# Bucketed attention into a capacity-routed mixture of experts: X's transposes in the maxima's tiles, sums of v in four column positions, and another order of the first expert's loads and subtractions

## The chip, the cores and the metric

One core of a Trainium2 chip runs the whole program. The metric is device time of one execution in microseconds, the median of several runs. TensorE (PE, with PEld for its weight loads), VectorE (DVE), ScalarE (ACT) and GpSimd (POOL) each work through their own queue in order; SyncE (SP) and GpSimd issue the DMAs.

## The reference

```python
def _attn_ref(q, k, v, proj):            # q, k, v: 4 x 8 x 768 x 64, proj: 64 x 6
    q_bits = (q @ proj > 0); k_bits = (k @ proj > 0)
    mask = q_bucket[..., :, None] == k_bucket[..., None, :]     # buckets: six bits each
    scores = np.where(mask, scale * q @ k.T, -1e9)
    attn = np.exp(scores - scores.max(-1, keepdims=True))
    return attn / (attn.sum(-1, keepdims=True) + 1e-9) @ v

def _moe_ref(x, w_gate, w1, w2):         # x: 3072 x 512, 8 experts, 512 -> 1024 -> 512
    # all (token, expert) logits are taken from the largest down; a token goes to the first
    # expert that still has room (384 each)
    out[mask] = np.maximum(x[mask] @ w1[e], 0) @ w2[e]
```

## The kernel before

**Attention.** The 32 heads (4 batches of 8) are taken in order, six key blocks of 128 each: 192 steps, numbered t. A step issues, in an order written out by hand, the transposed scores of one key block in two halves (`ST`, into a ring of three PSUM tiles `psT`, with the exponential on ScalarE), the row maxima of a later head (`S_pass`, into a ring of two tiles `psS` of two banks each, reduced on VectorE), the low halves of the probabilities (`lo`, mostly on GpSimd) and, four steps later, the product with v (`AV`). Everything in 32 bits is split into a high and a low half of 16. Other work is put into the steps by half-step numbers n = 2t: the lists `P1` to `P4` give the numbers at which the q, k and v of the next group of four heads are cast (`cast`, `cv`), subtracted (`sub`, `sv`), projected onto the hash bits (`bits`), moved by DMA to the layout that the scores use (`moves`) and summed over keys (`sumv`). For the second group (G=1) `moves` comes in three parts at half-steps 23, 24 and 28. The loads of a group's q and k go into tiles with one buffer, on SyncE's queue, which also issues the moves.

`sumv` multiplies a 128x128 matrix `on`, zero but for ones in two columns, with the 64 columns of v of four heads at once (256 columns, six blocks, high and low), so that rows 97 and 98 of one PSUM tile hold the sums; one copy on ScalarE and one operation on VectorE take rows 96 to 127 out.

After every second head `xtr` transposes its 128 columns of the attention's output X, three row blocks a call and two calls two half-steps apart, in tiles of `psT`; ScalarE copies the high half, VectorE subtracts the low one. `logits` multiplies them with the gate.

**Experts.** Each expert takes 68 pieces of matmuls: 32 of the first layer, 36 of the second (three blocks c of 128 members, twelve pieces each). Beside the pieces of one expert runs the routing of the next (`phase`), a chain of some ten to fourteen steps through VectorE and TensorE, put at piece numbers `E1`, `E2` and `EV`. The weights are gathered by GpSimd's indirect DMAs (`wload`), cast by ScalarE to their high half (`wsplit`), and the low half is subtracted in halves of a quarter, 128x512 each. These subtractions wait in a list `pend`: `hand` takes the next few of it at a routing step, behind a one-element copy (`tick`) that keeps GpSimd from running ahead of the step; the lists `hs` say how many at each step, and what has not been handed out by a piece number `by` is issued there. For the first expert the first half of w1 is loaded before the routing ends, the second half and w2 (two halves) behind a tick on the gathered and split X.

Of the kernel before, what the change touches and what calls it, by code (L numbers as in the profile page):

```python
# [27 lines left out]
 P1=[13, 14, 15, 16, 17, 18, 20, 21, 16, 24, 21, 26, 23, 24, 33, 32, 3, 2, 46, -1, -1, 13],  # L28
 P2=[41, 44, 48, 49, 51, 51, 57, 55, 45, 49, 55, 57, 52, 60, 59, 51, 1, 4, 63, 32, 36, 47],
 P3=[69, 73, 82, 80, 84, 86, 89, 86, 75, 83, 87, 90, 94, 96, 97, 99, 2, 3, 115, 58, 62, 87],  # L30
# [12 lines left out]
def attention(tc, nc, ctx, qT, kT, vv, proj, wg, x_dram, L, jp, identf, B, late=None, after=None):  # L43
# [64 lines left out]
    wc=row(97,768.0,"wc"); ml=row(98,-1.0,"ml")  # L108
    on=cp.tile([128,128],F16,name="on"); G_.memset(on,0.0); G_.memset(on[:,97:99],1.0)
    ident=cp.tile([128,128],F16,name="ident"); V.tensor_scalar(ident,jp,0.0,None,op0=ALU.is_equal)  # L110
# [51 lines left out]
    def moves(G,part=0):  # L162
# [4 lines left out]
        def go(dst,src,r0=0):  # L167
            for r,js in hs: SY.dma_start(dst[u][r0:r0+64,js,0:S],src[r])
# [7 lines left out]
        if part==1: todo=(go,QA,h[0]),(go,KA,h[1]),(signs_,)  # L176
        elif part==2: todo=(go,QB,h[0]),(nxt,0),(go,KB,h[1],64),(nxt,1)
        elif part==3: todo=()
        else: todo=(go,QA,h[0]),(go,QB,h[0]),(nxt,0),(go,KA,h[1]),(go,KB,h[1],64),(signs_,),(nxt,1)
        for f,*x in todo: f(*x)  # L180
        if part in (0,3): go(KB,l[1]); go(QB,l[0],64)
    def clear(G):
# [4 lines left out]
    def sumv(G):  # L187
        u=G%2
        if G<2:
            V.tensor_copy(WF[u][96:128,:,64],wc[96:128,:].to_broadcast([32,4]))  # L190
        ps=psT.tile([128,512],F32,name="pst")
        pv=ps[96:128,0:256].rearrange("p (j d) -> p j d",j=4)
        n=0
        for c in range(6):
            for src in (VH[u],VL[u]):
                T.matmul(ps[:,0:256].rearrange("p (j d) -> p j d",j=4),on,src[:,:,c,0:64],start=n==0,stop=n==11,skip_group_check=True); n+=1
        hi=dp.tile([128,4,64],F16,name="shi",bufs=1)
        A.copy(hi[96:128],pv)
        V.scalar_tensor_tensor(WF[u][96:128,:,0:64],hi[96:128],ml[96:128],pv,op0=ALU.mult,op1=ALU.add)

# [89 lines left out]
    def wsplit():  # L290
        A.copy(wgs[:,:,0],wgr); G_.tensor_tensor(wgs[:,:,1],wgr,wgs[:,:,0],op=ALU.subtract)
    def xtr(b,d,hf):
        ps=psT.tile([128,512],F32,name="pst"); p=ps[:,0:384].rearrange("p (c q) -> p c q",c=3); r=slice(3*hf,3*hf+3)
        for c in range(3):
            T.transpose(p[:,c],X[b][:,3*hf+c,d*128:d*128+128],identf)
        A.copy(XH[:,d,r],p)
        V.tensor_tensor(XL[:,d,r],p,XH[:,d,r],op=ALU.subtract)  # L297
# [49 lines left out]
    for h in range(1,NH,2):  # L347
        b,d=h//8,h%8//2; n=2*(6*h+5+LAG)+AP['X'][0]
        if h==NH-1: n=2*(6*h+5+LAG)
        for hf in range(2): add(n+AP['X'][1]*hf,xtr,b,d,hf)  # L350
        if b==B-1: add(n+4,logits,b,[d])
# [43 lines left out]
W2=[2,4,7,11]  # L395
W10=[(2,4),(3,6)]
W20=[9,12,15,18]
XS=[57,57,60,63]
# [3 lines left out]
class Moe:  # L402
# [399 lines left out]
    def start(s):  # L802
# [3 lines left out]
        next(s.ph0)  # L806
        s.gather(0)
        s.wsplit(0,0,0,V)
        next(s.ph0)
# [4 lines left out]
        s.gate=s.W[0,'x'][0][0:1,0,256:257].bitcast(F32); s.tick()  # L814
        s.wload(0,0,4,(2,3))
        s.wload(0,1,2)

    def run(s):
# [7 lines left out]
        for p in range(1,8):  # L826
# [3 lines left out]
            hs=[0]*(len(ev)-10)+HS  # L830
            if p==1: hs=[0,0,0,0,0,2,2,2,2,2,0,1,1,0]
            if p==2: hs=[0,2,3,2,3,2,0,0,4,0]
            if p==7: ev=ev[-2:]; hs=[0,0]
# [6 lines left out]
        for k in range(8):  # L840
            for q in range(4): add(NS*k+(W2 if k else W20)[q],s.wsplit,k,1,q,None,NS*k+(BY[2] if k else 42) if k<6 else 0)
            for n in SC: add(NS*k+n,s.scatter)
        for q,n in W10: add(n,s.wsplit,0,0,q,None,8*q-2)
        for n in range(-NS,NS*8):
# [59 lines left out]
```

## Time and profile before

| | |
|---|---|
| median of 3 runs | 765.25 us (764.78 to 770.71) |
| profiled execution | 768.65 us, of which the span of instructions is 766.8 |
| mean granted TensorE clock | 0.966 of full |
| TensorE busy | 698.3 us (91%) |
| VectorE busy | 562.9 us (73%) |
| GpSimd busy | 547.7 us (71%) |
| ScalarE busy | 403.2 us (53%) |

The profile is of one execution; its times run from the span's first instruction. A matmul's length includes its way through the array, so two matmuls in a row overlap: starts tell more than lengths. Attention ends at about 412 us, the first expert's matmuls begin at about 442 and the second's at about 490.

### The profile page before, as it was taken

Reading aid. Unit: us, or ns where it says so; the run is one execution under the profiler, and the core shown is the slowest. Engines: PE = TensorE matmul, PEld = TensorE weight load, DVE = VectorE, ACT = ScalarE, POOL = GpSimd, SP = SyncE. Lnnn points to the kernel's source line nnn. Section 1 sums busy time; section 2 is a strip of 40 time slices with the busy share of each in tenths; the row PEclk is TensorE's granted clock in tenths of the full one; section 3 lists DMA queues with packets and bytes.
Section 4 is the critical chain, followed back from the end, with each engine's and each line's share of the span. In section 5 each row is a group of like instructions: output and inputs, shape, how many; then the busy total and the mean of one; then the engine's idle time right before and its main releaser. Section 6 shows DMA issues by size and latency. Waiting matters only on the chain. (4 is left out here: it accounts for less than half of the span.)

```text
span 766.8 us, 19086 instructions
## 1 busy us (share of the span) xinstructions
PE 698.3 (91%) x7748; PEld 544.0 (71%) x7748; DVE 562.9 (73%) x1318; ACT 403.2 (53%) x788; POOL 547.7 (71%) x467
## 2 busy tenths in 40 slices
PE   7898898999999999998887687989999999999995
PEld 2566675767767676675665576877988888988894
DVE  6788978889888898987765687778888888843120
ACT  5776676777776777655562141614343434333430
POOL 7694969696886968765662375768787887887761
PEclk7899999999999999999997599999999999999998
DMA  8539655426454273420000343434262626262511
GB/s 206 147 96 220 149 157 123 121 74 166 129 122 123 80 190 98 105 58 23 22 22 23 97 166 111 165 138 151 86 217 77 227 67 237 59 244 97 207 39 42
DMA packets 40000, 93.57 MB, mean 122 GB/s; under 512 B 4597, under 2 KB 30569, under 8 KB 37865
## 3 DMA queue, kind: packets, MB, share of 16 engines
q1 hardware_dynamic: 33048, 46.21, 23.2%
q0 software_dynamic: 6784, 46.14, 17.2%
q8 instruction: 61, 1.00, 0.6%
q14 instruction: 27, 0.21, 0.1%
q10 hardware_dynamic: 80, 0.00, 0.0%
HBM read 59.53 MB, written 12.58 MB: 94 GB/s over the span
## 5 line engine op out<-in xcount | busy, mean ns | idle before, releaser
L258 POOL TENSOR_TENSOR lo<-pt 128x768 f16<-128x768 f32 x143 | 233.5, 1646 | 78.0 <-ACT pt L255 68.6
L255 ACT ACTIVATE pt<-pst 128x384 f32<-128x384 f32 x384 | 182.9, 491 | 98.6 <-PE pst L254 87.7
L231 DVE TENSOR_REDUCE m<-pss 128x1 f16<-128x770 f32 x192 | 182.6, 956 | 42.3 <-PE pss L229 41.3
L253 PE MATMUL pst<-qa,ka 128*128 128x384 f16 x384 | 125.6, 327 | 6.8 <-DVE XT L297 4.0
L254 PE MATMUL pst<-qb,kb 128*128 128x384 f16 x384 | 125.5, 327 | 1.1 <-DMA qb<-ql 1.1
L270 PE MATMUL psv<-vh,lo 128*128 128x65 f16 x1152 | 121.1, 194 | 1.8 <-POOL lo L258 1.8
L269 PE MATMUL psv<-vl,pt 128*128 128x64 f16 x1152 | 121.3, 193 | 0.0
L268 PE MATMUL psv<-vh,pt 128*128 128x65 f16 x1152 | 121.2, 194 | 0.0
L743 POOL TENSOR_TENSOR wl<-wf,wh 128x512 fp32r<-128x512 f32 x92 | 115.8, 1278 | 0.0
L268 PEld LDWEIGHTS <-pt 128*128 128x128 bf16 x1152 | 106.7, 98 | 12.7 <-issue 3.1
L269 PEld LDWEIGHTS <-pt 128*128 128x128 bf16 x1152 | 105.8, 99 | 9.5
L229 PE MATMUL pss<-ka,qa 128*128 128x385 f16 x384 | 95.4, 331 | 17.2 <-DVE m L231 14.6
L270 PEld LDWEIGHTS <-lo 128*128 128x128 f16 x1152 | 105.8, 97 | 2.0 <-POOL lo L258 1.9
L731 ACT CAST wh<-wf 128x1024 fp32r<-128x1024 f32 x64 | 65.1, 1048 | 38.3 <-DMA wf<-in_w_dram,zwidx 37.8
L779 ACT ACTIVATE hh<-ph 128x384 fp32r<-128x384 f32 x64 | 31.4, 491 | 83.3 <-PE ph L777 83.3
L229 PEld LDWEIGHTS <-qa 128*128 128x128 f16 x384 | 37.6, 98 | 50.4 <-issue 26.5
L780 DVE SCALAR_TENSOR_TENSOR hl<-ph,hh 128x384 fp32r<-128x384 f32 x64 | 35.3, 556 | 41.5 <-ACT hh L779 41.0
L777 PE MATMUL ph<-xh,wh 128*128 128x384 f32 x256 | 60.1, 349 | 3.3 <-DVE hl L780 3.0
L258 DVE TENSOR_TENSOR lo<-pt 128x768 f16<-128x768 f32 x49 | 61.6, 1258 | 1.5 <-ACT pt L255 1.0
L792 ACT COPY o<-po 128x512 f32<-128x512 f32 x24 | 14.1, 587 | 82.4 <-PE po L789 80.9
L777 PE MATMUL ph<-xl,wh 128*128 128x384 f32 x256 | 56.8, 340 | 0.0
L777 PE MATMUL ph<-xh,wl 128*128 128x384 f32 x256 | 56.1, 339 | 0.0
(263 smaller groups left out, 1418.1 us busy)
## 6 DMA issues: line engine op xcount, KB each, us to landing
vp<-in_vv_dram SPq DMA_DIRECT2D x8, 768.0 KB
x_dram<-X SPq DMA_DIRECT2D x16, 384.0 KB
qp<-in_qT_dram SPq DMA_DIRECT2D x7, 768.0 KB
kp<-in_kT_dram SPq DMA_DIRECT2D x7, 768.0 KB
qa<-qh SPq DMA_DIRECT2D x14, 192.0 KB
ka<-kh SPq DMA_DIRECT2D x14, 192.0 KB
qb<-qh SPq DMA_DIRECT2D x14, 192.0 KB
kb<-kh SPq DMA_DIRECT2D x14, 192.0 KB
```

Source lines behind the costliest of these rows:

```text
L229: T.matmul(ps[:,hf,0:HK],QA[u][:,j,qc*128:qc*128+128],KA[u][:,j,hf*HK:hf*HK+HK],start=True,stop=True)
L231: V.tensor_reduce(M6[h][:,qc:qc+1],ps[:,:,0:HK],axis=AX.XY,op=ALU.max,negate=True)
L253: T.matmul(ps[:,0:384],KA[u][:,j,kr],QA[u][:,j,r],start=True,stop=False)
L254: T.matmul(ps[:,0:384],KB[u][:,j,kr],QB[u][:,j,r],start=False,stop=True)
L255: A.activation(PT[h,kc][0][:,r],ps[:,0:384],AF.Exp,scale=0.125)
L258: eng.tensor_tensor(l,p,p.bitcast(BF)[:,1::2],op=ALU.subtract)
L268: T.matmul(av[:,c,:],ph[:,r],VH[u][:,j,kc,:],start=(kc==0 and c==0),stop=False,skip_group_check=True)
L269: T.matmul(av[:,c,0:64],ph[:,r],VL[u][:,j,kc,:],start=False,stop=False,skip_group_check=True)
L270: T.matmul(av[:,c,:],l[:,r],VH[u][:,j,kc,:],start=False,stop=False,skip_group_check=True)
L731: s.nc.scalar.copy(h[:,r],f[:,r])
L743: for _ in range(n): s.nc.gpsimd.tensor_tensor(*s.pend.pop(0)[1],op=ALU.subtract)
L777: T.matmul(p[:,0:384],a[:,o:o+128],b[:,d],start=n==0,stop=n==11)
```

## The change

In attention: `xtr2` takes all six row blocks of a pair of heads in one tile of `psS`, for the first three batches (twelve calls); the last batch keeps `xtr`. `sumv` uses a 128x32 matrix with ones in columns 1 and 2, and for each block one matmul for each head, in column position 32j, so that head j's sums stand in rows 32j to 32j+31 of 64 columns; the eviction is four copies and four operations. `moves` of the second group issues the high halves of q and k in its second part, then the low halves and after them the next group's loads in its third part. The numbers `P2` of the third group's casts and subtractions move by up to three half-steps.

In the experts: the second half of the first expert's w1 is loaded directly behind the gather of X, not behind the tick; its casts follow the split of X, and its subtractions keep their latest pieces 14 and 22. The splits of w2 are put three pieces earlier. The numbers of subtractions handed out at the steps of the second and the third expert's routing are changed.

```diff
- P2=[41, 44, 48, 49, 51, 51, 57, 55, 45, 49, 55, 57, 52, ...
+ P2=[43, 45, 47, 49, 51, 52, 53, 55, 47, 50, 54, 57, 52, ...
...
-    on=cp.tile([128,128],F16,name="on"); G_.memset(on,0.0); G_.memset(on[:,97:99],1.0)
+    on=cp.tile([128,32],F16,name="on"); G_.memset(on,0.0); G_.memset(on[:,1:3],1.0)
...
-        elif part==2: todo=(go,QB,h[0]),(nxt,0),(go,KB,h[1],64),(nxt,1)
-        elif part==3: todo=()
+        elif part==2: todo=(go,QB,h[0]),(go,KB,h[1],64)
+        elif part==3: todo=(go,KB,l[1]),(go,QB,l[0],64),(nxt,0),(nxt,1)
...
-        if part in (0,3): go(KB,l[1]); go(QB,l[0],64)
+        if part==0: go(KB,l[1]); go(QB,l[0],64)
...
-                T.matmul(ps[:,0:256].rearrange("p (j d) -> p j d",j=4),on,src[:,:,c,0:64],start=n==0,stop=n==11,skip_group_check=True); n+=1
+                for j in range(4): T.matmul(ps[32*j:32*j+32,0:64],on,src[:,j,c,0:64],start=n==0,stop=n==11,tile_position=(0,32*j),skip_group_check=True)
+                n+=1
...
-        A.copy(hi[96:128],pv)
-        V.scalar_tensor_tensor(WF[u][96:128,:,0:64],hi[96:128],ml[96:128],pv,op0=ALU.mult,op1=ALU.add)
+        for j in range(4):
+            A.copy(hi[96:128,j],ps[32*j:32*j+32,0:64])
+            V.scalar_tensor_tensor(WF[u][96:128,j,0:64],hi[96:128,j],ml[96:128],ps[32*j:32*j+32,0:64],op0=ALU.mult,op1=ALU.add)
...
+    def xtr2(b,d):
+        ps=psS.tile([128,2,512],F32,name="pss"); p=ps[:,:,0:384].rearrange("p z (c q) -> p z c q",c=3)
+        for c in range(6): T.transpose(p[:,c//3,c%3],X[b][:,c,d*128:d*128+128],identf)
+        h=XH[:,d].rearrange("p (z c) q -> p z c q",z=2); l=XL[:,d].rearrange("p (z c) q -> p z c q",z=2)
+        A.copy(h,p)
+        V.tensor_tensor(l,p,h,op=ALU.subtract)
...
-        for hf in range(2): add(n+AP['X'][1]*hf,xtr,b,d,hf)
+        if b<B-1: add(n,xtr2,b,d)
+        else:
+            for hf in range(2): add(n+AP['X'][1]*hf,xtr,b,d,hf)
...
-W10=[(2,4),(3,6)]
-W20=[9,12,15,18]
+W20=[6,9,12,15]
...
         s.gather(0)
+        s.wload(0,0,4,(2,3))
...
         s.gate=s.W[0,'x'][0][0:1,0,256:257].bitcast(F32); s.tick()
-        s.wload(0,0,4,(2,3))
         s.wload(0,1,2)
+        s.wsplit(0,0,2,by=14)
+        s.wsplit(0,0,3,by=22)
...
-            if p==1: hs=[0,0,0,0,0,2,2,2,2,2,0,1,1,0]
-            if p==2: hs=[0,2,3,2,3,2,0,0,4,0]
+            if p==1: hs=[0,0,0,1,0,2,2,2,2,2,1,0,0,0]
+            if p==2: hs=[0,1,2,2,2,3,0,1,5,0]
...
-        for q,n in W10: add(n,s.wsplit,0,0,q,None,8*q-2)
```

## Rows read from the trace of the kernel before

**Rows 1.** The busy time of each engine in three stretches of the span (the second batch to the end of the third in attention; expert 0; experts 1 to 7). Columns: stretch and its length, then busy us and instructions of each engine, the granted TensorE clock, the DMA engines' busy share, GB/s.

```profile
140.00:340.00 200.00, 191.55 (x2962) 140.95 (x2959) 172.67 (x242) 143.28 (x303) 154.78 (x117) 1.00 0.46 118
...
442.00:490.00 48.00, 41.49 (x296) 34.60 (x297) 36.02 (x151) 17.16 (x35) 31.09 (x33) 0.96 0.49 171
490.00:767.00 277.00, 262.96 (x1669) 228.97 (x1667) 168.94 (x596) 103.08 (x175) 206.44 (x193) 0.98 0.37 132
```

**Rows 2.** TensorE's groups of instructions in 140 to 340 us, shapes kept apart: line, engine, operation, names, shapes, count | busy us, mean ns of one | idle before.

```profile
L253 PE MATMUL pst<-qa,ka 128*128 128x384 f16 x205 | 66.7, 326 | 2.4 <-DVE XT L297 1.4 <-ACT pt L255 0.7 <-DVE Lm L306 0.2
...
L196 PE MATMUL pst<-vh,on 128*128 128x256 f16 x30 | 6.9, 274 | 0.0
```

**Rows 3.** TensorE in order of time at the sums of v of the sixth group: start, length, line, operation. The first two of twelve matmuls, and the score matmul that comes behind the twelfth.

```profile
235.12 0.27 PE L196 MATMUL pst<-vh,on 128*128 128x256 f16 x1
235.23 0.27 PE L196 MATMUL pst<-vl,on 128*128 128x256 f16 x1
...
236.44 0.32 PE L253 MATMUL pst<-qa,ka 128*128 128x384 f16 x1
```

**Rows 4.** TensorE in order of time where the program already uses four tile positions side by side, the projections of q and k onto the hash bits (32 columns of weights each). 78.05 is a pair of maxima matmuls ahead of them; the third row here is the fourth projection, the last row the fifth.

```profile
78.05 0.49 PE L229 MATMUL pss<-ka,qa 128*128 128x385 f16 x2
78.48 0.51 PE L141 MATMUL pss<-qp,pr 128*32 128x384 f32 x1
...
78.50 0.51 PE L141 MATMUL pss<-kp,pr 128*32 128x384 f32 x1
78.82 0.49 PE L141 MATMUL pss<-qp,pr 128*32 128x384 f32 x1
```

**Rows 5.** TensorE in order of time, the count of one routing round: 24 matmuls of 8 columns, each with weights of its own, one after another.

```profile
483.66 0.76 PE L511 MATMUL psa<-zOH,zcmp 128*128 128x8 bf16 x24
```

**Rows 6.** Groups of instructions over the span, shapes kept apart, of the sums' eviction (L198, L199) and of the smallest copies that ScalarE makes (L586).

```profile
L586 ACT ACTIVATE zE<-zD 128x24 bf16<-128x24 int32 x30 | 4.0, 210 | 0.9 <-DVE zcmp L500 0.9
...
L199 DVE SCALAR_TENSOR_TENSOR wf<-shi,ml,pst 32x256 f16<-32x256 f16 x8 | 3.9, 493 | 2.7 <-ACT shi L198 2.6
...
L198 ACT CAST shi<-pst 32x256 f16<-32x256 f32 x8 | 2.9, 364 | 9.0 <-PE pst L196 9.0
```

**Rows 7.** The same view, of the maxima (L231), of ScalarE's eviction of 768 columns (L239) and of the two evictions of X's transposes (L297, L296).

```profile
L231 DVE TENSOR_REDUCE m<-pss 128x1 f16<-128x770 f32 x192 | 182.6, 956 | 42.3 <-PE pss L229 41.3
...
L239 ACT ACTIVATE qa<-pss,mbi,msc 32x768 f16<-32x768 f32 x30 | 29.5, 983 | 10.5 <-PE pss L238 8.4
...
L297 DVE TENSOR_TENSOR XT<-pst,XT 128x384 f16<-128x384 f32 x32 | 17.4, 548 | 4.3 <-ACT XT L296 4.0
...
L296 ACT CAST XT<-pst 128x384 f16<-128x384 f32 x32 | 15.2, 479 | 5.7 <-PE pst L295 4.3
```

**Rows 8.** The tile XT between 40 and 345 us, who waited for its writers: us, times.

```profile
  PE pst L253: 4.0, 7
```

**Rows 9.** The list of waits over the span: who waited for whom, us in total, times, longest.

```profile
PE pss L229 <- DVE m L231: 14.6, 31, 1.5
```

**Rows 10.** In order of time, SyncE's queue, TensorE and GpSimd at the second group's low halves (qb<-ql is issued, who waits for it). In brackets: idle time before, and what ended it.

```profile
62.06 1.33 SPq L168 DMA_DIRECT2D qb<-ql  x2
...
74.86 0.32 PE L254 MATMUL pst<-qb,kb 128*128 128x384 f16 x1 [1.11 <-DMA qb<-ql]
...
75.68 1.64 POOL L127 TENSOR_TENSOR ql<-qp,qh 128x768 f16<-128x768 f32 x1 [9.00 <-DMA qb<-ql]
```

**Rows 11.** Busy time, clock and DMA, as in rows 1, of 55 to 75 us.

```profile
55.00:75.00 20.00, 16.00 (x226) 11.66 (x224) 17.17 (x23) 13.54 (x28) 10.33 (x7) 1.00 0.91 214
```

**Rows 12.** In order of time, GpSimd and TensorE at the end of expert 0's first block of the second layer (wl are the weights' low halves, which GpSimd subtracts).

```profile
468.41 1.27 POOL L743 TENSOR_TENSOR wl<-wf,wh 128x512 fp32r<-128x512 f32 x1
...
468.76 1.75 PE L789 MATMUL po<-wl,hh 128*128 128x512 f32 x7
...
473.14 1.25 POOL L743 TENSOR_TENSOR wl<-wf,wh 128x512 fp32r<-128x512 f32 x1
...
474.44 0.50 PE L789 MATMUL po<-wl,hh 128*128 128x512 f32 x1 [3.94 <-POOL wl L743]
```

**Rows 13.** Granted clock, as in rows 1, of 4 us stretches about the two gaps of TensorE.

```profile
472.00:476.00 4.00, 1.56 (x5) 1.15 (x5) 0.82 (x3) 0.58 (x1) 1.40 (x2) 0.87 0.81 336
476.00:480.00 4.00, 4.00 (x37) 3.19 (x36) 2.70 (x17) 0.96 (x2) 2.02 (x2) 0.70 0.41 152
...
504.00:508.00 4.00, 3.53 (x19) 3.09 (x20) 2.17 (x11) 0.00 (x0) 3.66 (x4) 0.71 0.00 0
```

**Rows 14.** In order of time, GpSimd, VectorE and TensorE in expert 1 (zd is a step of the third expert's routing).

```profile
499.75 3.75 POOL L743 TENSOR_TENSOR wl<-wf,wh 128x512 fp32r<-128x512 f32 x3
...
501.81 1.74 DVE L605 SCALAR_TENSOR_TENSOR zd<-zd,zn,zE 128x24 bf16<-128x24 bf16 x1
...
504.20 0.32 PE L518 MATMUL psa<-zOH,zcmp 128*128 128x32 bf16 x6 [1.96 <-DVE zcmp L500]
```

**Rows 15.** In order of time, VectorE and TensorE at the assignment of the second expert's members (zSTb is written, and read by the matmul that follows).

```profile
467.62 0.23 DVE L625 TENSOR_SCALAR zSTb<-ze,zcm 128x24 bf16<-128x24 f32 x1
...
468.06 0.20 PE L641 MATMUL psa<-zSTb,ntri 128*128 128x48 bf16 x1
```

**Rows 16.** In order of time, GpSimd and TensorE at the end of expert 1's first block of the second layer.

```profile
514.39 5.02 POOL L743 TENSOR_TENSOR wl<-wf,wh 128x512 fp32r<-128x512 f32 x4
...
517.59 2.38 PE L789 MATMUL po<-wl,hh 128*128 128x512 f32 x8
```

More of the change, by code (lines that the diff above doesn't have):

```diff
@@ L28 @@
  P1=[13, 14, 15, 16, 17, 18, 20, 21, 16, 24, 21, 26, 23, 24, 33, 32, 3, 2, 46, -1, -1, 13],
- P2=[41, 44, 48, 49, 51, 51, 57, 55, 45, 49, 55, 57, 52, 60, 59, 51, 1, 4, 63, 32, 36, 47],
+ P2=[43, 45, 47, 49, 51, 52, 53, 55, 47, 50, 54, 57, 52, 60, 59, 51, 1, 4, 63, 32, 36, 47],
  P3=[69, 73, 82, 80, 84, 86, 89, 86, 75, 83, 87, 90, 94, 96, 97, 99, 2, 3, 115, 58, 62, 87],
@@ L190, in sumv @@
             V.tensor_copy(WF[u][96:128,:,64],wc[96:128,:].to_broadcast([32,4]))
-        ps=psT.tile([128,512],F32,name="pst")
-        pv=ps[96:128,0:256].rearrange("p (j d) -> p j d",j=4)
-        n=0
+        ps=psT.tile([128,512],F32,name="pst"); n=0
         for c in range(6):
             for src in (VH[u],VL[u]):
-                T.matmul(ps[:,0:256].rearrange("p (j d) -> p j d",j=4),on,src[:,:,c,0:64],start=n==0,stop=n==11,skip_group_check=True); n+=1
+                for j in range(4): T.matmul(ps[32*j:32*j+32,0:64],on,src[:,j,c,0:64],start=n==0,stop=n==11,tile_position=(0,32*j),skip_group_check=True)
+                n+=1
         hi=dp.tile([128,4,64],F16,name="shi",bufs=1)
-        A.copy(hi[96:128],pv)
-        V.scalar_tensor_tensor(WF[u][96:128,:,0:64],hi[96:128],ml[96:128],pv,op0=ALU.mult,op1=ALU.add)
+        for j in range(4):
+            A.copy(hi[96:128,j],ps[32*j:32*j+32,0:64])
+            V.scalar_tensor_tensor(WF[u][96:128,j,0:64],hi[96:128,j],ml[96:128],ps[32*j:32*j+32,0:64],op0=ALU.mult,op1=ALU.add)
     def top(j):
```

## The prediction, made before the change was run

> **What bounds the kernel now.** I read the stretches first [rows 1], then TensorE's groups [rows 2], the waits [rows 8, 9], and last the engines in order of time around each place that the diff touches. In attention's steady part TensorE is busy 191.55 of 200 us, VectorE 172.67. Modelled ends flatter TensorE, so I look at starts: twelve sum matmuls take 235.12 to 236.44 with no gap, and score matmuls follow directly [rows 3]. Steps there take 200 us / (205/2) = 1.95 us [rows 2]. So in attention TensorE's queue sets the pace where it is dense, and what is taken off it counts nearly in full there; VectorE is a close second. In expert 0 TensorE is busy 41.49 of 48 us [rows 1]; the reader sees one hole of 3.94 us, ended by GpSimd's subtraction of a weight's low half [rows 12], and a lower clock behind it [rows 13]. Experts 1 to 7 are filled to 262.96 of 277 us; their one clear hole is 1.96 us in expert 1, with a late VectorE and a GpSimd that is subtracting [rows 14].
>
> **A, expert 0: about -4.0 us.** Twelve half subtractions of low halves are handed out one routing step at a time: ten in five pairs, then one at the step that ends with the members' running sum, one at the step that ends with the class counts. The last two start at 468.41 and 473.14, and TensorE's eighth low-half matmul stands until 474.44 [rows 12]. The change hands one out earlier (fourth of the routing's steps, ahead of the pairs), so the pairs hold numbers 2 to 11, and the twelfth goes at the step after them. It would start about where 468.41 stands now, or earlier, and be done by about 469.7, before the eighth matmul is due at 470.5 (468.76 + 1.75). The hole of 3.94 goes. Behind it the clock was at 0.87 and 0.70 of full in two slices of 4 us, in part at 1.2 GHz, not 2.4 [rows 13]: (1 - 0.70) x 4 = 1.2 us lost in the second and at most 0.5 in the first, of which I take 1.5 together. Together -5.4.
> Two things come back. The twelfth subtraction is one of 1.27 us [rows 12] and now runs while VectorE writes the assignment, which TensorE's next routing matmul reads with only about 0.2 us to spare (467.62 + 0.23, then 468.06) [rows 15]. VectorE can be held by a subtraction: one of its steps takes 1.74 us when three run on GpSimd beside it from 499.75 [rows 14]. I take 1.0 us, bounds 0 and 1.27. The early one, at the fourth step, stands ahead of the first digit's steps in the same way: 0.4, same bounds. Sum -5.4 + 1.4 = -4.0; ends -5.4 and -2.9.
> The third and fourth quarters of w1 now load before the tick on the gathered X, not after it, and both casts go into ScalarE's queue directly behind the split of X. GpSimd issues them in time in which it waits for that tick, and they share the DMA engines with the last gather; the second layer's weights then start about two issues earlier. I cost this at nothing: the cover is that the first layer is not short of these quarters before or after. Were a cast to wait for its load at the head of ScalarE's queue, the relu of the first blocks would stand behind it, and TensorE behind that.
>
> **B, expert 1: about -1.2 us.** Three subtractions at the fifth step become two. They end 1.25 earlier (3.75 / 3 [rows 14]), so the step of VectorE that now takes 1.74 us ends that much earlier, and the 1.96 us hole of TensorE shrinks to some 0.7. The clock of 0.71 in the 4 us behind it [rows 13] costs (1 - 0.71) x 4 = 1.2, which I take as given back. Against it: the last hand-out grows from four (5.02 us from 514.39) to five. It ended at 519.41 where TensorE's eight low-half matmuls, 517.59 to 519.97, were just being served [rows 16], so +1.25. The gathers for the next expert stand behind it on GpSimd, with the transposes still many matmuls away. Sum -1.25 - 1.2 + 1.25 = -1.2; ends -2.5 (the fifth finds slack) and +0.5 (the clock falls again behind the new hole).
>
> **C, sums of v: about -2.5 us.** Before, 12 matmuls of 256 columns at 0.11 us from start to start are 1.32 us of TensorE, eight times [rows 3]. After, 12 groups of four matmuls, 64 columns each, in four column positions. No row shows this shape. Lower end: four at once, 64 columns at the rate of rows 3 are 0.11/4 = 0.028, so 12 x 0.028 = 0.33. Upper end: one after another at the pace of small matmuls with weights of their own, (0.76 - 0.17)/23 = 0.026 (0.17 being an estimate of the last one's own length), so 48 x 0.026 = 1.23. The nearest row is the projections: four start within 0.02 us (78.48 to 78.50) and the next four 0.34 after the first [rows 4], so they do run side by side; I take 0.045 a group, 0.54. Going into the tiled form costs 78.48 - 78.05 - 2 x 0.165 = 0.10 there (two maxima matmuls of 385 columns, at 0.11 x 385/256 = 0.165); twice, in and out, 0.2. So 1.32 - 0.74 = 0.58 saved each. Six of the eight lie where TensorE is dense, and of these I count four fifths: 6 x 0.58 x 0.8 = -2.8.
> The eviction grows from one copy of 0.364 and one operation of 0.493 to four of each; with 64 columns each must be near the small copy, 0.21 [rows 6], though queued ones overlap. That is some +0.5 us each of ScalarE and VectorE per group, with VectorE waiting in turn for each copy, and the maxima and the next exponentials queued behind. ScalarE has room (143.28 of 200 [rows 1]); VectorE has less: +0.3 in all on the path, bounds 0 and 8 x 0.3 = 2.4. Sum -2.5; ends -6.3 (8 x (1.32 - 0.33 - 0.2)) and +3.3 (8 x (1.23 + 0.2 - 1.32) = 0.9 lost, and 2.4 of eviction).
> The Trainium skill, TensorE: Matmul & The Clock Gate, section on the 56 ns gap, says that starts of matmuls never come closer than about 25 ns, however few columns. By that, 48 would take 1.2 us and the sums would save nothing: C would be about +1 instead of -2.5. The projections' starts, four in 0.02 us, speak against it [rows 4]; the count's pace speaks for it [rows 5]. It is rival 1.
>
> **D, second group's moves: about -2.5 us.** SyncE now issues the high and low halves of that group first and the next group's q and k loads after. Before, the last low move was issued at 62.06, and its data had arrived only when TensorE's matmul started at 74.86 after 1.11 us of waiting, and GpSimd's subtraction at 75.68 after 9.00 [rows 10]; the engines of the DMA were 0.91 busy all that time [rows 11]. By the shapes in the code the two loads are 1.57 MB; at 214 GB/s they are 7.3 us that the low halves no longer queue behind. So both waits end. The direct price is 1.11; GpSimd's 9 us also put back the low halves of the probabilities that TensorE needs, and TensorE is idle 4.0 of 20 us there [rows 11], where the steady part has (200 - 191.55)/10 = 0.85 [rows 1]: 3.15 too much. Against it: q arrives about 7 us later, and its first cast, moved from half-step 41 to 43, is at the head of ScalarE's queue, where exponentials stand behind it; I set 0.65 against the gain. Ends -4 (all of that idle time) and +2 (no gain, and ScalarE's queue held for one step, 1.95).
>
> **E, transposes in the maxima's tiles: about +1.6 us.** Twelve times, two tiles of three blocks become one of six in the ring of two that the maxima use. The transposes stay. ScalarE pays 0.98 for 768 columns [rows 7] instead of 2 x 0.479; VectorE about 0.96, as a maximum of 770 columns does, instead of 2 x 0.548; the 0.14 that VectorE saves each time I cost at nothing, as it comes while TensorE is the later one. Gone are TensorE's waits for XT in the score ring, 4.0 us in 7 waits, if all of them fall on these twelve [rows 8]. New is that the next maxima matmul needs its predecessor's reduction done at once, since the transposes hold the other tile. That already happens with the rows of maxima in this ring: 14.6 us in 31 waits, 0.47 each [rows 9]; 12 x 0.47 = +5.6. Ends: 0, and one full reduction of 0.956 each, +11.5. Sum +1.6; ends -4.0 and +7.5.
>
> **Sum.** -4.0 - 1.2 - 2.5 - 2.5 + 1.6 = -8.6. Against the profiled execution's own 768.65 that is 760.05; it ran 3.4 over the median, so the forecast is 765.25 - 8.6 = 756.65.
>
> **The rivals.**
> 1, the sums gain nothing (48 starts one after another, C +1): -5.1, 760.15. For it rows 5, against it rows 4.
> 2, the experts give less: A at its poor end -2.9 and B at +0.5: -5.8, 759.45. For it: GpSimd's hold on VectorE [rows 14] and the thin margin [rows 15]; against it, that the hole itself is named by its releaser [rows 12].
> 3, slower: each of the twelve X tiles blocks the maxima's ring for a reduction and for the copy that VectorE waits for, in order, 0.956 + 0.983 = 1.94 us. E is then 23.3 - 4.0 = +19.3, the sum -10.2 + 19.3 = +9.1, 774.35. It turns slower from (10.2 + 4.0)/12 = 1.2 us a tile. Against it: VectorE has 27 of 200 us idle and the waits of that kind cost 0.47 so far [rows 1, 9].
> 4, attention gains more, as its dense stretches give each freed stall back whole: C -5, D -3, E -3 with A and B as above, -16.2, 749.05.
> 5, it does not do what it says: the ring of score tiles was not the limit and q's later load costs what the low halves gain; C, D and E together 0: -5.2, 760.05.
>
> **How the numbers follow.** Forecast 0.46, rival 1 0.12, rival 2 0.15, rival 3 0.06, rival 4 0.11, rival 5 0.10. The range 750 to 764 leaves out rival 3 and half of rival 4, and some of the forecast's tails. 1% is 7.65 us, about what a measurement of this kernel can tell from no change, so faster means below 757.6. Of the forecast's own 0.46 I put 0.36 there, with rival 4 0.11 and 0.05 from the better sides of rivals 1, 2 and 5: 0.52. Slower by 1% asks for over 772.9, most of rival 3: 0.05. The rest, 0.43, is the same.
>
> **What would show it.** A: no TensorE wait for wl in expert 0, clock 1.00 there, one pair of VectorE steps stretched about the assignment. B: the hole in expert 1 near 0.7 us, a wait for wl of about 1 us at its first second-layer block. C: four sum matmuls within 0.05 us, and the ScalarE wait for the sums (9.0 us [rows 6]) halved. D: no wait of GpSimd or TensorE for the second group's qb, perhaps one of ScalarE for q. E: no wait of scores for XT in the first three batches, more of maxima on VectorE. The prediction is wrong if the steps in attention stay at 1.95 us, or if the hole of expert 0 comes back elsewhere, as a wait of the first layer for a cast.

## The result and the profile after the change

The changed kernel is slower: 773.62 us (median of 20 runs, 769.27 to 776.83) against 766.90 for the kernel before in the same series (20 runs, 763.21 to 771.98). The ratio is 1.0084, with a 95% interval of 1.0065 to 1.0102: 6.4 us lost where 8.6 were to be gained, and outside the range of 750 to 764. The profiled execution took 770.54 us, its span 768.5.

The stretches of after, as in [rows 1] (stretch, length, busy us and instructions of PE, PEld, DVE, ACT and POOL, granted clock, DMA share, GB/s):

```profile
140.00:340.00 200.00, 180.44 (x2987) 130.59 (x2984) 168.39 (x236) 137.89 (x296) 146.87 (x113) 0.99 0.45 114
442.00:490.00 48.00, 41.93 (x317) 35.55 (x316) 39.73 (x153) 17.91 (x35) 29.87 (x32) 0.94 0.47 159
490.00:768.00 278.00, 265.28 (x1685) 230.88 (x1683) 172.39 (x609) 105.50 (x178) 208.45 (x196) 0.99 0.38 136
```

In attention TensorE has lost 11 us of busy time of 200, and VectorE, ScalarE and GpSimd have each lost some 4 to 8: nobody took over, everybody waits more. (Some of TensorE's 11 is work taken out, in the sums.) From the first matmul of expert 0 to the span's end it is the other way round: 442.10 to 766.8 before, 324.7 us; 448.40 to 768.5 after, 320.1. So the experts gained 4.6 and everything ahead of them lost 6.3, in these two executions. They differ by another 4.6 us before the first sums of v, which begin at 36.26 before and at 31.67 after, and in which the change has no part: over the traces of all the runs below that moment lies anywhere from 30.8 to 36.3, and at 30.9 and 35.4 for two kernels that are alike up to there (the moves with and without their new half-steps). (A part of it is ScalarE's idle time ahead of one early instruction, 5.64 us before and 3.20 after, for which the profile names no cause.) Counted from the first sums, attention and the switch to the experts lost 10.9 us and the experts gave 4.6 back: 6.3, near the measured 6.4. So further down the traces are compared from the first sums on.

The costliest groups of instructions say what the waiting is for (line, engine, operation, names, shapes, count | busy us, mean ns of one | idle just before, and what ended it):

```profile
L254 PE MATMUL pst<-qa,ka 128*128 128x384 f16 x384 | 125.5, 327 | 17.7 <-DVE wf L200 12.6
...
L200 DVE SCALAR_TENSOR_TENSOR wf<-shi,ml,pst 32x64 f16<-32x64 f16 x32 | 9.1, 284 | 7.5 <-ACT shi L199 7.4
L199 ACT CAST shi<-pst 32x64 f16<-32x64 f32 x32 | 6.5, 202 | 23.8 <-DVE wf L200 19.0 <-PE pst L195 4.8
```

L199 and L200 are the eviction of the sums of v, 32 instructions each instead of 8 [rows 6]. Their own time is small: 6.5 us on ScalarE instead of 2.9, 9.1 on VectorE instead of 3.9. But ScalarE stands idle for 19.0 us ahead of its copies until VectorE's operation on the part before is done, a wait that the kernel before did not have, and TensorE's scores stand for 12.6 us until the tile of sums is free (TensorE's waits for that tile do not show in the list of waits of the kernel before).

One group in order of time, the sixth (it begins at 235.12 here as in [rows 3]), TensorE first:

```profile
235.12 0.21 PE L195 MATMUL pst<-vh,on 128*32 128x64 f16 x4
235.16 0.42 PE L195 MATMUL pst<-vl,on 128*32 128x64 f16 x4
235.39 0.22 PE L195 MATMUL pst<-vh,on 128*32 128x64 f16 x4
...
235.64 0.21 PE L195 MATMUL pst<-vh,on 128*32 128x64 f16 x4
235.67 0.21 PE L195 MATMUL pst<-vl,on 128*32 128x64 f16 x4
237.29 0.32 PE L254 MATMUL pst<-qa,ka 128*128 128x384 f16 x1 [1.41 <-DVE Lm L314]
...
240.14 0.32 PE L254 MATMUL pst<-qa,ka 128*128 128x384 f16 x1 [1.16 <-DVE wf L200]
```

and ScalarE and VectorE behind it:

```profile
235.96 0.20 ACT L199 CAST shi<-pst 32x64 f16<-32x64 f32 x1 [0.57 <-PE pst L195]
238.45 0.20 ACT L199 CAST shi<-pst 32x64 f16<-32x64 f32 x1 [2.29 <-DVE wf L200]
239.00 0.20 ACT L199 CAST shi<-pst 32x64 f16<-32x64 f32 x1 [0.35 <-DVE wf L200]
239.56 0.20 ACT L199 CAST shi<-pst 32x64 f16<-32x64 f32 x1 [0.35 <-DVE wf L200]
239.78 0.49 ACT L256 ACTIVATE pt<-pst 128x384 f32<-128x384 f32 x1
```

```profile
233.56 1.78 DVE L186 TENSOR_TENSOR vl<-vp,vh 128x384 f16<-128x384 f32 x1
...
237.16 0.95 DVE L232 TENSOR_REDUCE m<-pss 128x1 f16<-128x770 f32 x1
238.14 0.28 DVE L200 SCALAR_TENSOR_TENSOR wf<-shi,ml,pst 32x64 f16<-32x64 f16 x1
238.69 0.28 DVE L200 SCALAR_TENSOR_TENSOR wf<-shi,ml,pst 32x64 f16<-32x64 f16 x1 [0.27 <-ACT shi L199]
239.24 0.28 DVE L200 SCALAR_TENSOR_TENSOR wf<-shi,ml,pst 32x64 f16<-32x64 f16 x1 [0.27 <-ACT shi L199]
239.79 0.29 DVE L200 SCALAR_TENSOR_TENSOR wf<-shi,ml,pst 32x64 f16<-32x64 f16 x1 [0.27 <-ACT shi L199]
```

The matmuls do what they were meant to: 48 of them start between 235.12 and about 235.70, and 0.2 us of that is a pause ahead of 235.39, until VectorE's subtraction of the low halves of v (vl) ends at 235.34. From 235.39 on a group of four starts every 0.031 us. The first copy is done at 236.16. VectorE, behind its maxima, comes to the first operation only at 238.14, and the second copy starts when that is over, at 238.45. From there copy and operation take turns, 0.55 us a pair. ScalarE's next exponential starts at 239.78; in the kernel before, where the sums began at the same 235.12, it started at 237.03:

```profile
236.64 0.36 ACT L198 CAST shi<-pst 32x256 f16<-32x256 f32 x1 [1.16 <-PE pst L196]
237.03 0.49 ACT L255 ACTIVATE pt<-pst 128x384 f32<-128x384 f32 x1
```

### The profile page after: what moved, and what is told of

It is laid out like the page before. It is cut to its first block, busy times and chain, and to the rows that moved or that the text cites. A ratio compares the mean times of both kernels' runs of the same rounds, so it can differ in the third digit from the quotient of the medians.

```text
span 768.5 us, 19696 instructions
## 1 busy us (share of the span) xinstructions
PE 690.1 (90%) x8036; PEld 536.8 (70%) x8036; DVE 571.7 (74%) x1330; ACT 406.1 (53%) x800; POOL 547.9 (71%) x468
## 5 line engine op out<-in xcount | busy, mean ns | idle before, releaser
L256 ACT ACTIVATE pt<-pst 128x384 f32<-128x384 f32 x384 | 182.4, 491 | 86.1 <-PE pst L255 73.5
L232 DVE TENSOR_REDUCE m<-pss 128x1 f16<-128x770 f32 x192 | 182.3, 955 | 35.8 <-PE pss L230 34.7
L254 PE MATMUL pst<-qa,ka 128*128 128x384 f16 x384 | 125.5, 327 | 17.7 <-DVE wf L200 12.6
L255 PEld LDWEIGHTS <-kb 128*128 128x128 f16 x384 | 37.5, 98 | 31.4 <-issue 19.6
## 6 DMA issues: line engine op xcount, KB each, us to landing
vp<-in_vv_dram SPq DMA_DIRECT2D x8, 768.0 KB
qp<-in_qT_dram SPq DMA_DIRECT2D x7, 768.0 KB
kp<-in_kT_dram SPq DMA_DIRECT2D x7, 768.0 KB
```

The lines of the kernel that those rows point to most:

```text
L232: V.tensor_reduce(M6[h][:,qc:qc+1],ps[:,:,0:HK],axis=AX.XY,op=ALU.max,negate=True)
L254: T.matmul(ps[:,0:384],KA[u][:,j,kr],QA[u][:,j,r],start=True,stop=False)
L255: T.matmul(ps[:,0:384],KB[u][:,j,kr],QB[u][:,j,r],start=False,stop=True)
L256: A.activation(PT[h,kc][0][:,r],ps[:,0:384],AF.Exp,scale=0.125)
```

## The experiments

Each gives the median, the ratio of its runs to those of the kernel before on the same chip, with a 95% interval, and the us by which it is slower (+) or faster (-): the ratio less 1, times the median of before beside it (766.5 to 768.0). The intervals reach 1.7 to 3.7 us to either side, and the difference of the two medians can lie up to 1.6 us from the figure given.

**Sums of v alone** (the kernel before with the new `on` and the new `sumv`).

> The kernel before with the sums of v in four column positions and their four-part eviction, nothing else of the change. Theory 1 (the eviction is the loss: each copy on ScalarE stands behind the VectorE operation of the part before it, and the score ring and the exponentials stand behind the copies): slower than before by 7 to 12 us; ScalarE waits for that operation some 19 us in 24 waits and TensorE for its tile about 11 us. Theory 2 (the sums are not the loss, the larger tile in the maxima's ring or the moved loads are): within 3 us of before.

775.11 us, 1.0124 (1.0076 to 1.0172): +9.5 us. The whole loss is in this part, and more than the whole. Its list of waits (who waited for whom: us, times, longest) shows the same two waits as the full change:

```profile
ACT shi L199 <- DVE wf L200: 15.7, 24, 2.2
PE pst L254 <- DVE wf L200: 11.8, 8, 2.5
```

**The full change with the old sums.**

> The changed kernel with the old sums of v (12 matmuls of 256 columns, one copy, one operation) put back. Theory 1: faster than before by 6 to 10 us (4.6 from the experts, as the two traces show, some 3 from the transposes, about 1 from the moves). Theory 2: not faster than before by more than 3 us, since its loss is still in it and takes the experts' gain away.

763.31 us, 0.9975 (0.9947 to 1.0002): -1.9 us. Without this part the change is at or slightly under the kernel before. That is not the 6 to 10 us of theory 1, and by this run alone theory 2 would stand; the run before it rules theory 2 out. What theory 1 had wrong here are the transposes and the moves, which do not give the 4 us that it counted for them (below).

**The full change, and sums alone, with all four copies ahead of the four operations.** The matmuls, the tile and the number of instructions stay:

```diff
-        for j in range(4):
-            A.copy(hi[96:128,j],ps[32*j:32*j+32,0:64])
-            V.scalar_tensor_tensor(WF[u][96:128,j,0:64],hi[96:128,j],ml[96:128],ps[32*j:32*j+32,0:64],op0=ALU.mult,op1=ALU.add)
+        for j in range(4): A.copy(hi[96:128,j],ps[32*j:32*j+32,0:64])
+        for j in range(4): V.scalar_tensor_tensor(WF[u][96:128,j,0:64],hi[96:128,j],ml[96:128],ps[32*j:32*j+32,0:64],op0=ALU.mult,op1=ALU.add)
```

> The changed kernel with the same instructions in the sums' eviction, but all four copies ahead of the four VectorE operations, so that no copy waits for VectorE. Theory 1: the 19 us of ScalarE's waits go, and with them most of the loss: 6 to 11 us faster than before. Theory 3 (the tiled matmuls themselves are dear, by the way into and out of the tiled form and the loads of weights): still within 3 us of the changed kernel, about 770.

> The kernel before with the sums in four column positions, all four copies ahead of the four operations. If only the order of the eviction was the loss: 1 to 4 us faster than before (the forecast's -2.5), so some 10 to 12 below the same without this order (775). If eight instructions instead of two are a cost of their own: 0 to 3 us slower.

The full change: 763.21 us, 0.9955 (0.9928 to 0.9983), -3.4 us, short of the expected 6 to 11, for the same reason. Sums alone: 766.02 us, 0.9974 (0.9950 to 0.9998), -2.0 us. In the second, ScalarE waits no more for VectorE here, and TensorE for 0.6 us instead of 11.8. Its sixth group on ScalarE and VectorE:

```profile
234.65 0.84 ACT L198 CAST shi<-pst 32x64 f16<-32x64 f32 x4 [0.36 <-PE pst L195]
235.52 0.49 ACT L255 ACTIVATE pt<-pst 128x384 f32<-128x384 f32 x1
```

```profile
234.59 0.95 DVE L231 TENSOR_REDUCE m<-pss 128x1 f16<-128x770 f32 x1
235.55 1.18 DVE L199 SCALAR_TENSOR_TENSOR wf<-shi,ml,pst 32x64 f16<-32x64 f16 x4
```

The order of two lines is worth 11.5 us in the sums alone (+9.5 to -2.0) and some 10 in the full change (+6.4 to -3.4); from the first to the eighth sums of v the two traces of the sums alone differ by 9.0 (302.5 and 293.5). VectorE's operations are as late behind the maxima as before, but now nobody but the tile stands behind them: the exponential starts 0.03 us after the last copy.

**The old matmuls with the new kind of eviction**, to part it from the tiled form:

```diff
-        A.copy(hi[96:128],pv)
-        V.scalar_tensor_tensor(WF[u][96:128,:,0:64],hi[96:128],ml[96:128],pv,op0=ALU.mult,op1=ALU.add)
+        for j in range(4):
+            A.copy(hi[96:128,j],pv[:,j])
+            V.scalar_tensor_tensor(WF[u][96:128,j,0:64],hi[96:128,j],ml[96:128],pv[:,j],op0=ALU.mult,op1=ALU.add)
```

> The kernel before with its twelve sum matmuls of 256 columns unchanged, and only the eviction cut into four pairs of a copy and an operation, of 64 columns each, taken in turn. Theory (ScalarE stands at the head of its queue for VectorE's operation, and the exponentials stand behind it): slower by 8 to 13 us, as much as the sums of v alone (+9.5) with the tiled matmuls' own gain of some 2 us taken out. Rival (the tiled matmuls or their switch of form cost the time): slower by 0 to 2 us, for the added instructions.

776.09 us, 1.0127 (1.0084 to 1.0170): +9.8 us. The tiled matmuls are not needed for the loss.

**Two copies, two operations, twice**, with the tiled matmuls: is it the number of returns or the time that ScalarE stands?

> The kernel before with the sums of v in four column positions, and the eviction as two copies, two operations, two copies, two operations: one return from ScalarE to VectorE's operations where the change has three. Theory (what costs is how long ScalarE's queue stands): the last copy would end at about 239.25 instead of 239.76, against 236.8 with all copies first, so (239.25 - 236.8) / (239.76 - 236.8) = 0.83 of the 11.5 us between +9.5 and -2.0 stay: +7.5 us. Rival (each return costs the same): a third of 11.5, less 2.0: +1.8 us.

775.12 us, 1.0104 (1.0069 to 1.0140): +8.0 us, the theory's +7.5. The one return left keeps most of ScalarE's wait, 10.7 us in 8. The run also tells what holds TensorE. In the change it was the tile of sums, which VectorE's last operation frees, so the late tile alone might have been the cost. Here that wait is down to 1.1 us, and nearly the whole loss stays: TensorE now waits 9.3 us for exponentials that stand behind the copies. Two pairs, then the kernel before:

```profile
ACT shi L199 <- DVE wf L200: 10.7, 8, 2.3
...
PE pst L254 <- ACT pt L256: 9.3, 11, 2.1
...
PE pst L254 <- DVE wf L200: 1.1, 1, 1.1
```

```profile
PE pst L253 <- ACT pt L255: 1.5, 4, 0.8
```

**The experts' part alone** (A and B).

> The kernel before with the experts' part of the change alone (loads, splits, hand-outs). All theories: attention as before, and the stretch from the first expert's first matmul to the end shorter by 4 to 5 us, as between the two traces (324.7 to 320.1 us); time 762 to 763. If what the experts give is lost at the switch from attention, within 2 us of before.

760.72 us, 0.9932 (0.9906 to 0.9958): -5.2 us. From the first expert's first matmul to the end it takes 319.7 us (324.7 before).

**X's transposes alone** (E).

> The kernel before with X's transposes in the maxima's tiles alone. After the first four runs the moves and this part together cost some 3 us (the changed kernel with the old sums is slower than the experts' part alone by 2.6). If the transposes are the cost (a maximum that waits for the tile, VectorE waiting for the longer copy): 2 to 5 us slower than before, TensorE's waits for maxima (14.6 us before) up by as much. If the end of the waits for XT (4.0 us) counts: 1 to 4 us faster.

769.70 us, 1.0030 (1.0000 to 1.0060): +2.3 us.

**The moves alone** (D, with the new half-steps `P2`).

> The kernel before with the second group's moves in the new order and the third group's new numbers alone. If q's later load is the cost: 2 to 4 us slower, with ScalarE waiting for the load. If the end of GpSimd's 9.00 us and TensorE's 1.11 us of waiting counts: 1 to 3 us faster.

767.00 us, 0.9998 (0.9975 to 1.0020): nothing, neither of the two. The four parts alone make +9.5 - 5.2 + 2.3 + 0 = +6.6, where the change measured +6.4; by their four intervals the sum is good to some 5 us, so that it fits so closely is chance.

**Where the moves' gain went.** I took the starts of the eight sums of v as marks. (Between the traces of before and of the experts' part alone, where attention is the same program, the marks from the second to the fourth differ by 0.3 and 0.5 us, those from the fourth to the eighth by 0.03.) From the second to the third is 21.1 us before (71.2 to 92.3) and 18.9 with the moves (70.4 to 89.3): 2.2 gained. From the third to the fourth it is 54.1 (to 146.4) and 56.4 (to 145.7): 2.3 lost. There GpSimd waits for the third group's low halves, which its next subtraction overwrites. First before, then with the moves alone:

```profile
108.19 1.64 POOL L127 TENSOR_TENSOR ql<-qp,qh 128x768 f16<-128x768 f32 x1 [4.56 <-DMA qb<-ql]
```

```profile
107.47 1.65 POOL L127 TENSOR_TENSOR ql<-qp,qh 128x768 f16<-128x768 f32 x1 [6.82 <-DMA qb<-ql]
```

Counted from the first sums (36.3 and 35.4) that wait ends at 71.9 and at 72.0. It comes at its own time, so GpSimd, arriving earlier, waits longer, and TensorE for GpSimd (1.65 us at 110.59, for the low half of the probabilities). With the casts at their old half-steps:

> The kernel before with the second group's moves and the next group's loads in the new order, and the third group's casts and subtractions at their old half-steps. With both the time was unchanged (0.0): 2.2 us gained up to the third sums of v, 2.3 lost between the third and the fourth, where GpSimd waits 6.8 us for the third group's low halves of q instead of 4.6. If the moved half-steps cause that wait: faster by 2 us. If the later loads cause it: within 1 us of the kernel before, or slower by up to 3, as the casts now wait for the loads at the head of ScalarE's queue.

765.01 us, 0.9974 (0.9941 to 1.0006). The interval does not tell this from nothing. The trace does: the wait is 6.5 us, ends 71.8 after the first sums, and the third and fourth sums are 56.0 apart. The moved half-steps are not the cause. In the kernel before, SyncE's queue holds these low halves back behind the eight sign moves and the load of the next k:

```profile
98.73 0.66 SPq L173 DMA_DIRECT2D ka<-bt  x1
99.50 0.38 SPq L58 DMA_DIRECT2D kp<-in_kT_dram  x1
99.93 2.27 SPq L168 DMA_DIRECT2D kb<-kl  x2
102.24 1.49 SPq L168 DMA_DIRECT2D qb<-ql  x2
```

Two kernels change that queue for the third group only, on top of the moves with old half-steps:

```diff
+        elif G==2: todo=(go,QA,h[0]),(go,QB,h[0]),(nxt,0),(go,KA,h[1]),(go,KB,h[1],64),(go,KB,l[1]),(go,QB,l[0],64),(signs_,),(nxt,1)
...
+        elif G==2: todo=(go,QA,h[0]),(go,QB,h[0]),(nxt,0),(go,KA,h[1]),(go,KB,h[1],64),(signs_,),(go,KB,l[1]),(go,QB,l[0],64),(nxt,1)
```

> The kernel before with the second group's moves in the new order (casts at their old half-steps), and for the third group alone the moves of the low halves put ahead of the eight sign moves and of the load of the next k. Theory (SyncE's queue gives the second group's gain back, because the third group's low halves stand behind the sign moves until some 64 us after the first sums): GpSimd's wait for them, 6.5 us, goes, and the 2.2 us stay gained: 2 to 4 us faster than the kernel before. Rival (something else sets the pace there, or the later sign moves now hold the maxima's operands): within 1 us, or slower by some 2 us.

> The same with the third group's low halves behind the sign moves and ahead of the load of the next k only. If that load, which the low halves queue behind in the DMA engines, sets the time: 2 to 3 us faster than the kernel before, as with the moves ahead of the signs. If the sign moves do: the wait shrinks by some 1 to 3 of 6.5 us, and the time is 0 to 1.5 us under the kernel before.

Ahead of the signs: 763.81 us, 0.9934 (0.9901 to 0.9968), -5.1 us. Behind the signs, ahead of the load: 762.12 us, 0.9933 (0.9904 to 0.9963), -5.1 us. Both are more than was expected, within their intervals. Third to fourth sums take 51.4 and 52.9 us, where the moves with the old half-steps took 56.0. In the first GpSimd waits for no low half:

```profile
101.53 1.64 POOL L127 TENSOR_TENSOR ql<-qp,qh 128x768 f16<-128x768 f32 x1
```

In the second 3.3 us of that wait stay, worth 1.5 us by the marks, which the runs do not show. So it is the load of the next k, ahead of the low halves, that took the gain back, as 3.2 us by the marks come with its place alone: the same fault that the change removed in the second group, one group later. How much the third group's new order gives without the second group's was not run; in the kernel before GpSimd waits 4.56 us there too.

**The best of it.** Experts' part and sums with copies first:

> The experts' part and the sums with the copies first, neither moves nor transposes. If the parts add up: the experts' -5 and the sums' -1 to -4, so 757 to 761, the fastest so far. If the sums give nothing: 761 as the experts alone.

762.06 us, 0.9915 (0.9889 to 0.9941), -6.5 us. Other hand-outs on top of it (2 at the second expert's fourth step and none behind the pairs; 2, 2, 2, 2, 3, 0, 1, 4, 0 for the third's):

> The fastest kernel so far (the experts' part of the change and the sums with all copies first, -6.5 us) with other numbers of subtractions handed out: 2 instead of 1 at the fourth step of the second expert's routing and none after the pairs; 2, 2, 2, 2, 3 and at the end 1 and 4 instead of 1, 2, 2, 2, 3, 1 and 5 in the third's. If the waits seen with the change (1.05 us behind the assignment in expert 0, 1.7 us for the low halves in expert 1) are the hand-outs' doing: 1 to 2.5 us faster than -6.5. If they only move: the same as it, or slower by 1 to 3 us as the early steps of the routing are held instead.

762.42 us, 0.9935 (0.9907 to 0.9962), -5.0: no gain that can be told. The wait of 0.83 behind the assignment in expert 0 is gone and two of the three for low halves in expert 1 (1.0 together), but the first count of expert 1 waits 0.98 instead of 0.51. With the second group's moves, and with these and the third group's low halves ahead of the signs:

> The experts' part of the change, the sums of v with all copies first, and the second group's moves in the new order with the casts at their old half-steps. The parts add up so far (-5.2, -2.0, and 0 to -2.0): -6.5 if the moves give nothing, -8.5 if they give 2.0.

> The same with the third group's low halves ahead of the sign moves. If SyncE's queue gave the gain back: 2 to 4 us faster than the kernel with the experts' part and the sums with copies first, -8.5 to -10.5 against the kernel before. If not: -6.5, or less.

762.63 us, 0.9936 (0.9909 to 0.9962), -4.9, where -6.5 or -8.5 was expected; and **757.31 us, 0.9855 (0.9813 to 0.9897), -11.1** (-10.1 by the two medians). The last beats both kernels. The second group's moves show a gain clear of the intervals only together with the third group's.

## Why the prediction was wrong

**C, sums of v: the step that failed, forecast -2.5, measured +9.5.** Its price for the matmuls was about right, a little high. Forecast 0.54 + 0.2 us a group, gain 0.58. Measured with copies first, where seven of the eight groups start without a pause: 12 x 0.031 = 0.37 for the matmuls, 0.09 on the way in (in the sixth, 234.02 - 233.60 - 2 x 0.165) and 0.12 on the way out (in the second, where the last four start at 69.18 and the next score at 69.33): 0.58 in all, a gain of 0.74. Rival 1 fell with it. The Trainium skill, TensorE: Matmul & The Clock Gate, section on the 56 ns gap, has about 25 ns as the least from start to start, by which 48 would take 1.2 us, an estimate; the trace disagrees for matmuls side by side, with some 8 ns each.

But that four fifths of this come off the time is not shown. With copies first the part gave -2.0 (-3.8 to -0.2), near the forecast, and added to the full change's other parts or to the experts' part it took 1.5 and 1.3 us off, within the noise. In the trace the fourth to the eighth sums take 182.4 us with it and 182.3 before, where 4 x 0.74 = 3.0 of TensorE's time went: in this stretch TensorE's queue alone does not set the pace. What does is open; VectorE's operations on the sums grew by 0.65 us a group (9.1 instead of 3.9 us in eight).

The term that failed is the eviction, "+0.3 in all on the path, bounds 0 and 2.4". It counted the added instructions (0.202 and 0.284 us each now, about as forecast; queued, they do not overlap as it said, four copies take 0.84) and named one wait, VectorE's for each copy, with maxima and exponentials queued behind. It did not ask what the second copy waits for. In program order a copy follows the operation of the part before, both read the tile of sums and both name the tile `shi`, and in the changed kernel each of the three later copies waits for that operation, though neither reads what the other writes. The operation stands behind VectorE's maxima (2.29 us at 238.45), and behind the copy stand ScalarE's exponentials, which make the probabilities. The prediction had the rows for it: VectorE is the second-busiest engine in this stretch [rows 1], its maxima take 0.956 each [rows 7]. ScalarE's room, which it cited, is no help when ScalarE's queue is held. 11.5 us are shown for the order (copies first or in turn; some 10 in the full change), 9.8 for the eviction without the tiled matmuls, and that the time the queue stands counts, not the turns, by the two pairs. Where copies and operations go singly in turn, the tile of sums comes free (240.08) shortly before the next exponential is done (239.78 + 0.49), so there the two cannot be told apart; that the held queue is enough for the loss, the two pairs show. Through which tile the order comes, that of sums or `shi`, no run here tells.

The Trainium skill, PSUM — Partial Sum Buffer, section on bank collisions, says that ScalarE and VectorE must not both access one bank of PSUM within the same 32 partitions at once, reads included, but that different groups of 32 partitions of a bank may go together. By that, the new layout (head j in partitions 32j to 32j+31) needed no order between a copy and the operation on another part. In the trace they were ordered all the same (24 waits for 24 later copies), just as in the kernel with all parts in partitions 96 to 127 (24 waits, 11.2 us). What the layout allows and what a program orders are two questions.

**A and B, experts: right, -5.2 forecast, -5.2 measured (-7.2 to -3.2).** The 3.94 us hole of expert 0 [rows 12] is gone, and the clock from 472 to 488 is 1.00, where 0.87 and 0.70 stood in eight of these us [rows 13]. The price came where it was expected, at the assignment; then expert 1's:

```profile
460.65 0.32 PE L527 MATMUL psa<-zOH,zcmp 128*128 128x32 bf16 x6 [1.09 <-DVE zcmp L509]
...
476.32 0.20 PE L650 MATMUL psa<-zSTb,ntri 128*128 128x48 bf16 x1 [1.05 <-DVE zwidx L715]
...
519.72 0.50 PE L798 MATMUL po<-wl,hh 128*128 128x512 f32 x1 [0.26 <-POOL wl L752]
520.95 0.50 PE L798 MATMUL po<-wl,hh 128*128 128x512 f32 x1 [0.73 <-POOL wl L752]
522.17 0.63 PE L798 MATMUL po<-wl,hh 128*128 128x512 f32 x1 [0.72 <-POOL wl L752]
```

1.05 at the assignment against 1.0; 1.09 at a count in the digit steps, 0.5 more than in the kernel before, where 0.4 was set for the early hand-out; 0.26 + 0.73 + 0.72 = 1.71 for the fifth subtraction against 1.25. Of the hole that B shrank, 1.96 [rows 14], 0.45 is left (506.20), but the count ahead of it now waits too, 0.76 (502.73). Behind the three waits for low halves the clock of this execution is 0.80 and 0.77 from 520 to 528, as the poor end of B had it; in the trace of the experts' part alone, with the same three waits, it stays at 1.00.

**D, moves: forecast -2.5, measured 0.** The step itself was right: neither TensorE's 1.11 nor GpSimd's 9.00 us [rows 10] is left, and the third sums came 2.2 us earlier. What the prediction set against it, q's cast at the head of ScalarE's queue, was not the price (ScalarE waits 0.5 us for that load). It did not look one group further, where the low halves have a time of their own; rival 5 had the outcome, with the wrong reason.

**E, transposes: forecast +1.6, measured +2.3 (0 to 4.6), but not by its terms.** The waits for XT in the score ring (4.0 us [rows 8]) are gone, as said. The +5.6 of maxima waiting for their ring did not come:

```profile
PE pss L229 <- DVE m L231: 15.7, 31, 1.5
```

This is the kernel with the transposes alone, +1.1 against [rows 9]. By the marks it gains 2.9 us from the second to the third sums (18.2 for 21.1), where two of the seven waits for XT stood, 1.6 us. From the third to the fourth it loses 1.9 of them (56.0 for 54.1): GpSimd's subtraction there waits 6.66 us instead of 4.56 (the profile names a cast of k as its end, of which it reads nothing) and starts 71.6 us after the first sums, as in the kernel before (71.9), so the gain seems to end at the same low halves as that of the moves; no run takes that wait away beside the transposes. From the fourth to the eighth sums it loses 1.0 (183.3 for 182.3), with VectorE waiting 3.4 us in 6 for ScalarE's copy of 0.799. Another 3.4 us of its profiled execution lie between the last sums and the first expert; 20 us there ran at a clock of 0.93, which is at most 1.4, and for kernels that are alike in this stretch it differs by 2.0 from trace to trace. Two terms were wrong and cancelled, so the nearness of forecast and measurement is luck; what the rest of the cost is stays open.

Rival 3 had nearly the measured time, 774.35, and that too is luck: its cause, the transposes at +19.3, measured +2.3.

The range failed with C alone: its end for the eviction was set from instruction times, +2.4, and the cost of a queue that is held was not among the bounds.

## What to carry to other kernels

When an eviction is cut into parts that go through two engines, write all of the first engine's instructions ahead of the second's, and ask of each added instruction not only what its own result waits for but what its engine's queue waits for while it stands at the head. A wait of a lightly used engine for a heavily used one costs what is queued behind it. Time taken off the busiest engine is not yet time taken off the kernel: here 0.74 us a group of TensorE's went, and the marks did not move. And a gain from an earlier transfer lasts only as far as the next transfer with a time of its own: look one round further before counting it.

## What the runs showed of the hardware

Matmuls of 64 columns on 128x32 weights in four column positions started a group of four every 0.031 us, some 8 ns a start (0.34 us from the first to the twelfth group, in seven of eight sums of the kernel with copies first); the way into that form took 0.09 us and the way out 0.12. Four copies of 32x64 queued on ScalarE took 0.84 us together (0.202 each alone) and four operations on VectorE 1.18 (0.284), so cutting an eviction in four costs some 0.5 and 0.7 us where nothing waits in between. And the place of one load in a queue reached further than its own group: the next k's load, issued 0.43 us ahead of the third group's low halves (99.50 and 99.93), undid the 2.2 us gained in the second; with it behind them the third to fourth sums took 1.2 to 2.7 us less than the 54.1 of before.
